# Last block's stores on ScalarE with halved copies, second loads chained from the third batch on, and a new table of priorities

## The chip, the cores and the metric

One core of one Trainium2 chip runs the whole kernel. The metric is the device time in microseconds. Shares and instruction times come from one profiled execution.

## The reference

Two stages follow each other. The first is a gated linear attention over 4 batches, 8 heads, 768 steps and 48 channels; the second takes its output, as 4 x 768 rows of 384, through a product, a three-tap convolution with a sigmoid gate, and a second product.

```python
# attention, per batch and head
for t in range(S):
    cur = (u * k_t) outer v_t
    y_t = r_t @ (state + cur)
    state = w_t[:, None] * state + k_t outer v_t
# second stage: x is y with heads side by side, (4, 768, 384)
h = relu(x @ w_in)                       # w_in 384 x 1024
c = sum over j of conv_w[j] * h shifted by j - 1 along the sequence
out = (h * sigmoid(c)) @ w_out           # w_out 1024 x 384
```

The three weights arrive as 8-byte floats.

## The kernel before

**Tiling.** The attention goes in 24 chunks of 128 steps, six for each batch. `loads` fetches a chunk's w, k, r and v on SyncE's queue (line 613); `stage_a` transposes them on TensorE (645), scans the decays on VectorE (654, 662), forms products on GpSimd (692, 694) and turns the keys back (712). `stage_b` does the state work of a chunk on TensorE: the carried part (771), the scores (803), the update (813) and the part within (781). ScalarE copies the result into `xT` (863), VectorE writes the remainder beside it (865), and after a batch's fourth and sixth chunk SyncE moves the spare rows into place with six transfers each time (874).

**Blocks.** The second stage goes in eight blocks of 384 rows, two for each batch. For each of eight f, `block` runs nine matmuls (885), then the steps of `gating`: ScalarE 897, 898, 903, 906, VectorE 899, 901, 904, GpSimd 907. The values stand in `gh` tiles, three f to a tile. Then 24 matmuls (914) for each of three output tiles sum over f; in the last block the order of those is by f first and by output tile second. A copy (945) and a store (946) end each output tile.

**Weights.** GpSimd fetches `w_in` by indirect transfers (571), SyncE loads `w_out` (584), and `from_double` and `convert` turn the words into 4-byte values with VectorE (522, 525), ScalarE (520, 542) and GpSimd (528, 543).

**Second loads for the word checks.** `again` loads the weights a second time in six pieces (602) on ScalarE's queue, and `small_words` reads each with two ScalarE operations (534) that sum up words outside the range that the fast path is made for, into the tile `flags`. Lines 1058 to 1062 turn all sums into one number, `inside`: a reduction on VectorE, a matmul on TensorE, a comparison on VectorE. Each engine then loads that number (1066) and branches (1067) over a slow path that is there for unusual inputs.

**The order** is made by `Plan`: each piece of work is handed to `op` with an engine, a length from `LEN`, what it reads and writes, and a rank. `Plan.issue` walks through a simulated time; when an engine is free it takes the ready operation with the least rank. The rank is a number for the chunk or block plus entries of the table `SHIFT`, one for the stage (`a1`, `i7`, `w1`) and one for the stage's letter with the operation's kind (`wfetch`, `pwts`, `ascan`). The result is one fixed sequence for each engine. Tiles with few copies are places of a `Kind`; `gh` tiles and the raw tiles of weights share a ring of five permits, and `Kind.take` holds a place back for a kind that still has tiles to come:

```python
kept = sum(max(0, min(o.keep - o.held, o.wanted - o.served)) for o in self.kinds if o is not self)
if self.held >= self.cap or len(self.places) <= kept:
    return None
```

Of the kernel before, what the change touches and what calls it, by code (L numbers as in the profile page):

```python
# [43 lines left out]
    fill=0.17, kh=0.335, guard=0.62, sbd=0.34, xhi=0.49, relu=0.5, mul=0.47, sig=0.43, cast=0.41, out=0.36, exp=0.46,  # L44
    z=1.03, zh=0.73, dsel=0.6, diag=1.07, lo=0.97,
    words=1.28, top=0.1, sdl=0.27, fetch=1.1, gather=1.6, rest=0.3, carried_rows=1.4, y_rows=1.5, ones=0.8,
    load=0.78, issue=0.55, spread=0.73,
)
SHAPE = dict(cross=3, half=3, output=3, scores=1, state=2, y=2, state_y=2, y_rows=2)
TURN = dict(tr=0.18, kback=0.18, carried=0.18)  # L50
PAUSE = 0.08
SHIFT = dict(
    a1=486, a10=10, a11=-18, a12=1721, a13=-81, a14=373, a15=1550, a16=-5, a17=-2983, a19=60, a2=-187, a21=-120,
    a22=-359, a23=-323, a3=564, a4=-460, a5=2857, a6=-907, a7=26, a8=-1139, adg=2121, adsel=469, afill=-1128,
    agather=278, aguard=-10, akback=101, akh=236, akt=-56, aones=259, ascan=8, asmall=202, aspread=80, atop=1,
    atr=6061, az=192, azh=-1916, b0=293, b1=54, b10=172, b11=311, b12=-289, b13=205, b14=-397, b16=-43, b17=-125,
    b18=422, b19=72, b2=8, b20=-384, b21=-277, b23=-27, b24=571, b3=-36, b4=114, b5=-77, b6=179, b8=-463, b9=123,
    bcph=2596, bcross=123, bhalf=477, boutput=378, bs=3878, bsa=-378, bsd=-16, bsdl=365, bsmall=10, bspread=-21,
    bxhih=-35, bxloh=-4306, c=-10, cexp=97, cfill=-99, cissue=-266, clo=239, ctr=191, cwords=-316, cwstt=-125,
    cwts=-21, i0=-310, i2=438, i3=-28, i5=-331, icast=-1967, igate=-1561, imm3=3579, imul=-1362, irelu=285, isig=-154,  # L60
    istt=1127, k=-26, kissue=225, ksmall=-331, l0=-133, l1=55, l11=147, l12=-694, l13=-381, l14=143, l16=-331,
    l18=213, l19=-23, l2=-167, l20=1132, l21=35, l22=-131, l23=-75, l3=-175, l4=-219, l5=-37, l7=19, l8=-366, l9=146,
    lload=5054, o0=-231, o1=195, o2=-305, o3=135, o4=-32, o5=-160, o6=-14, o7=61, oissue=-72, omm3=8366, oout=-13,
    p0=-400, p1=-1988, p10=-778, p11=-1950, p12=-115, p13=-232, p14=-285, p15=589, p16=-556, p2=16, p3=-496, p4=5592,
    p5=162, p6=315, p7=29, p9=125, pcast=963, pexp=-965, plo=-954, pwstt=1024, pwts=1129, q0=995, q2=-301, q3=1717,
    q4=-5, q5=-10, qissue=-174, qwords=273, w1=-800, w2=105, w3=606, w6=-356, wfetch=285, wissue=-178,
)
TAIL = dict(PE=0.22, DVE=0.11, ACT=0.13, POOL=0.07, SP=2.3, LOAD=1.8)
BEGIN = dict(PE=4.3, DVE=3.0, ACT=3.2, POOL=8.3, SP=0.8)
# [77 lines left out]
class Plan:  # L147
# [6 lines left out]
    def op(self, eng, us, f, r=(), w=(), holds=(), moves=0.0, port=False, rank=None):  # L154
        i, deps = len(self.ops), set()
        self.tags.append((self.stage, self.stage[0] + us))
        self.what.append(us)
        us = LEN[us] if isinstance(us, str) else us
        for t in r:
            if t in self.last:  # L160
                deps.add(self.last[t])
            self.readers.setdefault(t, []).append(i)
        for t in w:
            if t in self.last:
                deps.add(self.last[t])
            deps.update(self.readers.get(t, ()))
            self.last[t], self.readers[t] = i, []
        deps.discard(i)
        bufs = []
        for t in (*r, *w, *holds):  # L170
            if isinstance(t, Buf) and t not in bufs:
                bufs.append(t)
                t.uses += 1
                if t.turn is None:
                    t.turn = t.kind.wanted
                    t.kind.wanted += 1
        self.ops.append((eng, us, f, deps, bufs, moves, port,
                         (self.rank if rank is None else rank) + sum(SHIFT.get(x, 0) for x in self.tags[i]) + i * 1e-6))
# [191 lines left out]
def rwkv_conv_moe_kernel(  # L370
# [12 lines left out]
    nc = tc.nc  # L383
    B, H, S, D = r.shape
    DM, DF = w_in.shape
# [4 lines left out]
    NCH = S // L  # L390
# [3 lines left out]
    KT = DM // P  # L394
# [5 lines left out]
    N = B * NCH  # L400
# [48 lines left out]
    for m in range(KT):  # L449
        for g in range(2):  # L450
            half, r0 = rows_of[m][64 * g:64 * g + 64], (6 + g) * D + 16 * m - D
# [51 lines left out]
    op = plan.op  # L503
# [27 lines left out]
    def small_words(raw, buf, k, n, reads, rows=P):  # L531

        for j, kind in enumerate((U32, I32)):
            op("ACT", "words", lambda j=j, kind=kind: nc.scalar.activation(
                out=raw()[:, 0:2 * n:2].bitcast(F32), in_=raw()[:, 1:2 * n:2].bitcast(kind), func=AF.Relu, scale=-2.0 ** -30,
                bias=small_lo[0:rows, j:j + 1], accum_out=flags[0:rows, N + 2 * k + j:N + 2 * k + j + 1]),
                reads, [buf, ("flag", N + 2 * k + j)])
# [53 lines left out]
    def again(k):  # L591

        raw, n = Buf(raw_k), DF if k < KT else min(3, FT - 3 * (k - KT)) * DM

        def words():
            return raw.t.rearrange("p j c -> p (j c)")[:, 0:2 * n]
        if k < KT:
            rows, source = words, w_in[k * P:(k + 1) * P, :]
        else:
            t = 3 * (k - KT)  # L600
            rows, source = lambda: raw.t[:, 0:n // DM, :], w_out[t * P:t * P + n // DM * P, :].rearrange("(t p) c -> p t c", p=P)
        op("ACT", "issue", lambda: nc.scalar.dma_start(out=rows(), in_=source), [("x", (B - 1) % 2, NCH - 1, j) for j in range(10)], [(raw, 0)], [raw], moves=(0.0027 * n, 309.0 if k < KT else 122.0, 8))
        small_words(words, raw, k, n, [(raw, 0)])


# [275 lines left out]
    def product_in(t, f, m, x0, xs, wi=wi):  # L881

        j = 0
        for (a, c) in ((0, 0), (0, 1), (1, 0)):
            nc.tensor.matmul(t.t[:, 0:HB + 2], lhsT=wi[:, m, a, f * P:(f + 1) * P], rhs=xT[:, x0 + m, c, xs],  # L885
                             start=(m == 0 and j == 0), stop=(m == KT - 1 and j == 2))
            j += 1
# [24 lines left out]
    def product_out(acc, part, f, tt):  # L912
        for (a, c) in ((0, 0), (0, 1), (1, 0)):
            nc.tensor.matmul(acc.t[:, 0:DM], lhsT=part(a)[:, tt * P:(tt + 1) * P], rhs=wo[:, f, c, :],  # L914
                             start=(f == 0 and a + c == 0), stop=(f == FT - 1 and a == 1))

    def block(b, s0, width, base, last):
        xs = slice(s0, s0 + width + 2)
        x0 = (KT + 1) * (b % 2)
        xr = [("x", b % 2, c, j) for c in range(max(0, s0 - 1) // L, min(s0 + width, S - 1) // L + 1) for j in range(10)]  # L920
        gs = []
        for f in range(FT):
            plan.rank, plan.stage = base + f * UNIT, f"i{b * NB + s0 // HB}"
            t, a1, g = Buf(mm), Buf(a1_k), Buf(g_k)
            if f % 3 == 0:
                gh = Buf(gh_k)
            for m in range(KT):
                f0 = f * P // HB * HB
                op("PE", "mm3", lambda t=t, f=f, m=m: product_in(t, f, m, x0, xs),
                   [*xr, ("wi", m, f0), (("wi", m, f0), 1)], [t])  # L930
            key, part = ("gh", b, s0, f), lambda a, gh=gh, f=f: gh.t[:, f % 3, a, :]
            for j, (e, us, fn, rd, wr) in enumerate(gating(t, a1, g, part, f, width, key)):
                op(e, us, fn, rd, wr, [gh] if j > 5 else [], port=(e == "POOL"))
            gs.append((gh, key, part))
        plan.stage = f"o{b * NB + s0 // HB}"
        for tt in range(width // P):
            acc = Buf(mo)
            for f in range(FT):
                plan.rank = base + FT * UNIT + (f * 3 + tt if last else tt * FT + f) * DOWN
                gh, key, part = gs[f]  # L940
                op("PE", "mm3", lambda acc=acc, f=f, tt=tt, part=part: product_out(acc, part, f, tt),
                   [key, (key, 1), ("wo", f), (("wo", f), 1)], [acc], [gh])
            o = Buf(val_k)
            rows = slice(s0 + tt * P, s0 + (tt + 1) * P)
            op("ACT", "out", lambda acc=acc, o=o: nc.scalar.copy(out=o.t, in_=acc.t[:, 0:DM]), [acc], [o])
            op("SP", "issue", lambda o=o, rows=rows: nc.sync.dma_start(out=out[b, rows, :], in_=o.t), [o], [], moves=(0.6, 62.0, 8))

# [75 lines left out]
    for n in range(N + 1):  # L1023
# [29 lines left out]
    inside = const.tile([1, 1], I32, name="inside")  # L1053
# [7 lines left out]
       ["fsum"], [total])  # L1061
    op("DVE", "small", lambda: nc.vector.tensor_scalar(
        out=inside, in0=total.t[0:1, 0:1], scalar1=0.0, scalar2=None, op0=ALU.is_le), [total], ["inside"])
    plan.issue()
    fast.close()
    flag = nc.values_load(inside, min_val=0, max_val=1)
# [32 lines left out]
```

## Time and profile before

| what | us |
|---|---|
| time, median of 3 runs (342.13 to 344.29) | 343.53 |
| the profiled execution's time | 342.58 |
| its span, first to last instruction | 340.9 |
| TensorE, VectorE, ScalarE, GpSimd busy | 314.6, 262.9, 223.6, 184.1 |
| end of the last matmul for an output | 332.76 |

The time stands 1.7 us above the span. Names in the rows: PE is TensorE, PEld its weight load, DVE VectorE, ACT ScalarE, POOL GpSimd, SP SyncE; a q behind an engine's name is its queue, with transfers, waits, loads of a number and branches, which are not counted as busy. PEclk is TensorE's granted clock as a share of full speed.

### The profile page before, as it was taken

What the parts mean: (1) busy time and instruction counts of PE and PEld (TensorE: products, weight loads), DVE (VectorE), ACT (ScalarE), POOL (GpSimd) and SP (SyncE); (2) the same over time, 40 slices, a digit from 0 to 9 for tenths busy, and PEclk for the clock granted to TensorE, in tenths of its full rate; (3) what the DMA queues carried; (4) which work ended last, traced back from release to release, by engine and by line L of the source; (5) the groups of instructions that cost most, each with busy time, mean ns of one, the idle gap of its engine ahead of it and who ended that gap; (6) DMA issues with size and microseconds to landing.
All of it is one profiled execution on the core that took longest, in us unless ns stands there. A gap on an engine that the chain in (4) does not pass through costs nothing.

```text
span 340.9 us, 11473 instructions
## 1 busy us (share of the span) xinstructions
PE 314.6 (92%) x4510; PEld 294.6 (86%) x4510; DVE 262.9 (77%) x620; ACT 223.6 (66%) x587; POOL 184.1 (54%) x242
## 2 busy tenths in 40 slices
PE   8858858789999999999999999999999999999990
PEld 3846646689999999999999999999999999999990
DVE  5899998999999787698986867899998547554500
ACT  4266545987877643678866534878856348898780
POOL 8978983997674961247844621547733303413320
PEclk9998995799999999999999999999999999999996
DMA  8989864663371364368243633664501323534522
GB/s 158 322 283 213 217 168 88 127 122 66 75 155 44 84 129 102 62 125 170 65 94 77 145 52 97 129 123 104 122 17 50 91 42 125 166 126 162 180 98 79
DMA packets 114467, 41.37 MB, mean 121 GB/s; under 512 B 103117, under 2 KB 110822, under 8 KB 113638
## 3 DMA queue, kind: packets, MB, share of 16 engines
q1 hardware_dynamic: 112468, 31.14, 41.4%
q10 hardware_dynamic: 1506, 6.29, 5.4%
q0 software_dynamic: 432, 3.15, 2.4%
q8 instruction: 36, 0.59, 0.7%
q14 instruction: 25, 0.20, 0.2%
HBM read 31.48 MB, written 4.72 MB: 106 GB/s over the span
## 4 chain that ended last, share of the span: by engine, by line
PE 77%; DVE 7%; DMA 5%; POOL 3%; ACT 2%; SPq 2%; issue 1%; POOLq 0%
PE bank L914 30%; PE bank L885 28%; PE bank L645 5%; PE bank L771 3%; PE bank L781 3%; DMA gh<-in_moe_w_in_dram,limits 3%; PE bank L803 3%; PE bank L813 2%; DMA w<-in_w_dram 2%; PE bank L712 2%; POOL wide L528 1%; SPq L688 1%; DVE kr L662 1%; DVE kr L654 1%; DVE wide L525 1%
## 5 line engine op out<-in xcount | busy, mean ns | idle before, releaser
L914 PE MATMUL bank<-wo,gh 128*128 128x384 f32 x576 | 117.4, 345 | 0.0
L907 POOL TENSOR_TENSOR gh<-g,gh 128x384 fp32r<-128x384 f32 x64 | 64.7, 1018 | 95.4 <-ACT gh L906 94.7
L885 PE MATMUL bank<-xT,wi 128*128 128x386 f32 x576 | 111.3, 345 | 1.2 <-DVE xT L865 0.6
L885 PEld LDWEIGHTS bank<-xT,wi 128*128 128x128 f32 x576 | 102.8, 191 | 2.6 <-DVE kr L662 1.0
L914 PEld LDWEIGHTS bank<-wo,gh 128*128 128x128 f32 x576 | 99.0, 188 | 0.8
L899 DVE SCALAR_TENSOR_TENSOR a<-bank,cw,a 128x384 f32<-128x384 f32 x64 | 38.9, 611 | 21.4 <-ACT a L898 20.8
L897 ACT ACTIVATE bank<-bank 128x386 f32<-128x386 f32 x64 | 30.5, 481 | 23.6 <-PE bank L885 22.7
L904 DVE TENSOR_TENSOR g<-bank,a 128x384 f32<-128x384 f32 x64 | 35.0, 550 | 11.5 <-POOL gh L907 10.3
L704 POOL TENSOR_SCALAR_AFFINE_SELECT pm<-dg 64x512 f32<-64x512 f32 x46 | 30.2, 656 | 19.0 <-PE bank L781 14.1
L901 DVE SCALAR_TENSOR_TENSOR a<-bank,cw,a 128x384 f32<-128x384 f32 x64 | 38.7, 608 | 1.1 <-DVE sd L739 0.4
L906 ACT CAST gh<-g 128x384 fp32r<-128x384 f32 x64 | 32.1, 514 | 10.5 <-DVE g L904 9.7
L898 ACT ACTIVATE a<-bank,cw 128x384 f32<-128x384 f32 x64 | 37.0, 583 | 2.5 <-DVE dA L659 1.4
L903 ACT ACTIVATE a<-a 128x384 f32<-128x384 f32 x64 | 33.6, 525 | 7.3 <-DVE a L901 6.2
L692 POOL TENSOR_TENSOR z<-r,k 128x384 f32<-128x384 f32 x24 | 24.3, 1013 | 17.4 <-issue 6.1
L654 DVE TENSOR_TENSOR_SCAN kr<-bank,one_end 128x387 f32<-128x387 f32 x24 | 22.9, 956 | 4.2 <-POOL kr L480 2.7
L863 ACT CAST xT<-bank 112x256 fp32r<-112x256 f32 x48 | 16.1, 377 | 14.5 <-PE bank L781 14.3
L694 POOL TENSOR_TENSOR z<-z,ubc 128x384 f32<-128x384 f32 x24 | 24.3, 1014 | 1.0
L771 PE MATMUL bank<-kr,sa 48*48 48x64 f32 (+1 forms) x288 | 21.1, 232 | 2.5 <-DVE bank L828 1.1
L662 DVE TENSOR_TENSOR_SCAN kr<-bank,dA 128x387 f32<-128x387 f32 x24 | 22.9, 953 | 0.1
L771 PEld LDWEIGHTS bank<-kr,sa 48*48 48x48 f32 (+1 forms) x288 | 14.8, 129 | 8.4 <-issue 3.5
L528 POOL TENSOR_TENSOR wide<-wide,wide 128x384 int32<-128x384 int32 (+2 forms) x18 | 16.6, 929 | 7.2 <-DVE wide L525 6.7
L841 DVE COPY_PREDICATED pm<-upper_half,bank 128x256 f32<-128x256 int32 x48 | 20.0, 442 | 0.6 <-POOL pm L704 0.6
(106 smaller groups left out, 546.8 us busy)
## 6 DMA issues: line engine op xcount, KB each, us to landing
w<-in_w_dram SPq DMA_DIRECT2D x24, 192.0 KB, 3.5
k<-in_k_dram SPq DMA_DIRECT2D x24, 192.0 KB, 3.4
r<-in_r_dram SPq DMA_DIRECT2D x24, 192.0 KB, 3.5
v<-in_v_dram SPq DMA_DIRECT2D x24, 192.0 KB, 3.8
out_dram<-wide SPq DMA_DIRECT2D x24, 192.0 KB, 3.0
gh<-in_moe_w_in_dram ACTq DMA_DIRECT2D x3, 1024.0 KB, 4.8
gh<-in_moe_w_out_dram SPq DMA_DIRECT2D x2, 1152.0 KB, 6.3
gh<-in_moe_w_out_dram ACTq DMA_DIRECT2D x2, 1152.0 KB, 5.2
```

The source lines that it names most:

```text
L704: op("POOL", "zh", lambda p=slice(HL * j, HL * (j + 1)): nc.gpsimd.affine_select(out=pm.t[p].rearrange("p g m t -> p (g m) t"), in_=dg.t[p ...
L771: nc.tensor.matmul(to(h, m, c, w), lhsT=q["sa" if h else "sd"].t[p, m, 0:w], rhs=rt(out_of, m)[p, HL * h:HL * (h + 1)], start=first(h, c), ...
L885: nc.tensor.matmul(t.t[:, 0:HB + 2], lhsT=wi[:, m, a, f * P:(f + 1) * P], rhs=xT[:, x0 + m, c, xs], start=(m == 0 and j == 0), stop=(m == ...
L897: ("ACT", "relu", lambda: nc.scalar.activation(out=h(0, width + 2), in_=h(0, width + 2), func=AF.Relu), [t], [t]),
L898: ("ACT", "mul", lambda: nc.scalar.mul(out=a(), in_=h(1), mul=cw[:, 1, bass.ds(f, 1)]), [t, "cw"], [a1]),
L899: ("DVE", "stt", lambda: nc.vector.scalar_tensor_tensor(out=a(), in0=h(0), scalar=cw[:, 0, bass.ds(f, 1)], in1=a(), op0=ALU.mult, op1=ALU. ...
L901: ("DVE", "stt", lambda: nc.vector.scalar_tensor_tensor(out=a(), in0=h(2), scalar=cw[:, 2, bass.ds(f, 1)], in1=a(), op0=ALU.mult, op1=ALU. ...
L903: ("ACT", "sig", lambda: nc.scalar.activation(out=a(), in_=a(), func=AF.Sigmoid), [], [a1]),
L904: ("DVE", "gate", lambda: nc.vector.tensor_tensor(out=g.t[:, 0:width], in0=h(1), in1=a(), op=ALU.mult), [t, a1], [g]),
L906: ("ACT", "cast", lambda: nc.scalar.copy(out=part(0)[:, 0:width], in_=g.t[:, 0:width]), [g], [key]),
L907: ("POOL", "lo", lambda: nc.gpsimd.tensor_tensor(out=part(1)[:, 0:width], in0=g.t[:, 0:width], in1=part(0)[:, 0:width].bitcast(F32), op=AL ...
L914: nc.tensor.matmul(acc.t[:, 0:DM], lhsT=part(a)[:, tt * P:(tt + 1) * P], rhs=wo[:, f, c, :], start=(f == 0 and a + c == 0), stop=(f == FT ...
```

## The change

The last block's three output tiles are copied in halves, columns 0 to 191 by ScalarE and 192 to 383 by VectorE, and ScalarE issues their stores in place of SyncE. The second loads wait for the last chunk of the third batch, in place of the fourth; from the second of them on each waits also for the second word operation of the one before. LEN gets lengths for the new kinds of operation, and an operation `after` on GpSimd's list, which issues nothing, follows `inside`. All values of SHIFT are new.

```diff
-    load=0.78, issue=0.55, spread=0.73,
+    load=0.78, issue=0.55, outh=0.23, send=0.36, after=3.0, spread=0.73,
...
 SHIFT = dict(
-    a1=486, a10=10, a11=-18, a12=1721, a13=-81, a14=373, a15=1550, a16=-5, a17=-2983, a19=60, a2=-187, a21=-120,
...
-    agather=278, aguard=-10, akback=101, akh=236, akt=-56, aones=259, ascan=8, asmall=202, aspread=80, atop=1,
...
-    p0=-400, p1=-1988, p10=-778, p11=-1950, p12=-115, p13=-232, p14=-285, p15=589, p16=-556, p2=16, p3=-496, p4=5592,
-    p5=162, p6=315, p7=29, p9=125, pcast=963, pexp=-965, plo=-954, pwstt=1024, pwts=1129, q0=995, q2=-301, q3=1717,
-    q4=-5, q5=-10, qissue=-174, qwords=273, w1=-800, w2=105, w3=606, w6=-356, wfetch=285, wissue=-178,
+    a0=-2743, a1=1205, a10=-1850, a11=-18, a12=-6, a13=282, a14=-2337, a15=341, a16=-576, a17=-44, a18=-40, a19=93,
...
+    afill=-419, agather=102, aguard=-486, akback=1290, akh=-1246, akt=-1343, aones=-131, apad=292, ascan=140,
...
+    oissue=1003, omm3=7616, oout=-662, oouth=36, p0=-49, p10=25, p11=-97, p12=-110, p13=-148, p14=257, p15=-16,
+    p16=-26, p3=65, p4=3558, p5=-2, p6=138, p8=208, pcast=283, pexp=-1847, plo=73, pwstt=122, pwts=640, q0=-475,
+    q1=-334, q3=132, q4=1, q5=-1, qissue=-479, qwords=357, w1=-512, w3=437, w4=-1220, w5=381, w6=7, wfetch=-1128,
+    wissue=-42,
 )
...
-        op("ACT", "issue", lambda: nc.scalar.dma_start(out=rows(), in_=source), [("x", (B - 1) % 2, NCH - 1, j) for j in range(10)], [(raw, 0)], [raw], moves=(0.0027 * n, 309.0 if k < KT else 122.0, 8))
+        op("ACT", "issue", lambda: nc.scalar.dma_start(out=rows(), in_=source), [("x", (B - 2) % 2, NCH - 1, j) for j in range(10)] + [("flag", N + 2 * k - 1)] * (k >= 1), [(raw, 0)], [raw], moves=(0.0027 * n, 309.0 if k < KT else 122.0, 8))
...
             o = Buf(val_k)
             rows = slice(s0 + tt * P, s0 + (tt + 1) * P)
+            if last:
+                half = DM // 2
+                op("ACT", "outh", lambda acc=acc, o=o: nc.scalar.copy(out=o.t[:, 0:half], in_=acc.t[:, 0:half]), [acc], [o])
+                op("DVE", "outh", lambda acc=acc, o=o: nc.vector.tensor_copy(out=o.t[:, half:DM], in_=acc.t[:, half:DM]),
+                   [acc], [(o, 1)], [o])
+                op("ACT", "send", lambda o=o, rows=rows: nc.scalar.dma_start(out=out[b, rows, :], in_=o.t), [o, (o, 1)], [],
+                   moves=(0.6, 62.0, 8))
+                continue
...
+    op("POOL", "after", lambda: None, ["inside"], [])
     plan.issue()
```

## Rows read from the trace of the kernel before

**Rows 1.** The page's first part, busy us of each engine and instructions.
```profile
PE 314.6 (92%) x4510; PEld 294.6 (86%) x4510; DVE 262.9 (77%) x620; ACT 223.6 (66%) x587; POOL 184.1 (54%) x242
```

**Rows 2.** Table by stretch: length, busy us by engine, granted clock, DMA share, GB/s.
```profile
core 0: us, PE busy (x) PEld busy (x) DVE busy (x) ACT busy (x) POOL busy (x), PEclk, DMA share, GB/s
...
40.00:60.00 20.00, 14.28 (x238) 11.45 (x236) 17.50 (x47) 11.10 (x39) 13.46 (x18) 0.83 0.63 143
60.00:80.00 20.00, 17.37 (x325) 16.05 (x326) 19.16 (x48) 17.92 (x51) 19.85 (x22) 0.91 0.55 108
...
280.00:300.00 20.00, 20.00 (x116) 20.00 (x115) 12.74 (x24) 17.07 (x38) 7.06 (x7) 1.00 0.46 147
```

**Rows 3.** Chain of waits in order of time: start, us, what, near its end.
```profile
316.55 15.37 PE bank L914 x87
332.03 0.73 PE bank L914 x3
```

**Rows 4.** TensorE's groups by line from 275.75 to 332.8 us.
```profile
L914 PE MATMUL bank<-wo,gh 128*128 128x384 f32 x178 | 33.4, 338 | 0.0
L885 PE MATMUL bank<-xT,wi 128*128 128x386 f32 x144 | 27.1, 339 | 0.0
```

**Rows 5.** Timeline of the end: start, us, engine, line, operation, idle before.
```profile
332.07 0.15 DVE L1062 TENSOR_SCALAR inside<-bank 1x1 int32<-1x1 f32 x1 [1.41 <-PE bank L1060]
332.79 0.48 ACT L945 COPY wide<-bank 128x384 f32<-128x384 f32 x1 [0.35 <-PE bank L914]
```

**Rows 6.** Line 946's instructions (ns, first and last start) and landings, last and all.
```profile
L946 SPq DMA_DIRECT2D out_dram<-wide x1: 332/332/332, 333.3 to 333.3; - x1
...
DMA to landing us min/median/max: 3.8/3.8/3.8
...
DMA to landing us min/median/max: 1.9/3.0/5.7
```

**Rows 7.** Line 1067's instructions on SyncE's and VectorE's queues.
```profile
L1067 SPq EVENT_SEMAPHORE  x8: 17/17/17, 337.8 to 338.3; - x8
...
L1067 DVEq COMPARE_BRANCH  x1: 72/72/72, 332.9 to 332.9; - x1
...
L1067 SPq COMPARE_BRANCH  x1: 50/50/50, 334.6 to 334.6; - x1
L1067 DVEq EVENT_SEMAPHORE  x1: 21/21/21, 335.8 to 335.8; - x1
```

**Rows 8.** Line 1094's instructions, SyncE's next eight waits and ScalarE's joining.
```profile
L1094 SPq EVENT_SEMAPHORE  x8: 17/28/28, 338.4 to 338.9; - x8
...
L1094 ACTq EVENT_SEMAPHORE  x1: 17/17/17, 340.2 to 340.2; - x1
```

**Rows 9.** Lines 863 and 850: copies out of a bank, ns least, median, most.
```profile
L863 ACT CAST xT<-bank x48: 357/378/391, 23.1 to 274.8; 112x256 fp32r<-112x256 f32 x48
...
L850 DVE COPY sa<-bank x4: 344/346/346, 15.6 to 216.1; 112x192 f32<-112x192 f32 x4
```

**Rows 10.** Line 602's issues (ns, first and last start) and their landings.
```profile
L602 ACTq DMA_DIRECT2D gh<-in_moe_w_in_dram x3: 335/341/367, 282.2 to 294.9; - x3
...
DMA to landing us min/median/max: 4.8/5.2/6.7
```

**Rows 11.** Line 534's word operations on the second loads.
```profile
L534 ACT ACTIVATE gh<-gh,limits x12: 978/1258/1377, 289.6 to 329.3; 128x1024 f32<-128x1024 uint32 x3, 128x1024 f32<-128x1024 int32 x3, 128x1152 f32<-128x1152 uint32 x2, 128x1152 f32<-128x1152 int32 x2
L534 ACT ACTIVATION_READ_ACCUMULATOR gh<-gh,limits x12: 185/190/248, 290.8 to 330.2; 128x1 f32 x12
```

**Rows 12.** Line 874's spreads from 215 to 225 us.
```profile
L874 SPq DMA_DIRECT2D xT<-xT x6: 586/596/1167, 219.3 to 223.4; - x6
```

**Rows 13.** Waits of TensorE to 75 us and of its weight loads after.
```profile
PE bank L645 <- ACT w L639: 4.7, 3, 2.9
...
PEld bank L771 <- issue: 3.3, 14, 0.3
```

**Rows 14.** Table by stretch around 65 us, columns as in rows 2.
```profile
60.00:65.00 5.00, 3.36 (x84) 3.03 (x85) 4.72 (x11) 4.88 (x16) 5.00 (x6) 0.66 0.95 188
65.00:70.00 5.00, 4.96 (x90) 4.61 (x80) 5.00 (x14) 4.97 (x14) 5.00 (x6) 1.00 0.17 35
```

More of the change, by code (lines that the diff above doesn't have):

```diff
@@ L52 @@
 SHIFT = dict(
-    a1=486, a10=10, a11=-18, a12=1721, a13=-81, a14=373, a15=1550, a16=-5, a17=-2983, a19=60, a2=-187, a21=-120,
-    a22=-359, a23=-323, a3=564, a4=-460, a5=2857, a6=-907, a7=26, a8=-1139, adg=2121, adsel=469, afill=-1128,
-    agather=278, aguard=-10, akback=101, akh=236, akt=-56, aones=259, ascan=8, asmall=202, aspread=80, atop=1,
-    atr=6061, az=192, azh=-1916, b0=293, b1=54, b10=172, b11=311, b12=-289, b13=205, b14=-397, b16=-43, b17=-125,
-    b18=422, b19=72, b2=8, b20=-384, b21=-277, b23=-27, b24=571, b3=-36, b4=114, b5=-77, b6=179, b8=-463, b9=123,
@@ L58 @@
[L58 to L62, printed above, removed]
@@ L63 @@
-    lload=5054, o0=-231, o1=195, o2=-305, o3=135, o4=-32, o5=-160, o6=-14, o7=61, oissue=-72, omm3=8366, oout=-13,
-    p0=-400, p1=-1988, p10=-778, p11=-1950, p12=-115, p13=-232, p14=-285, p15=589, p16=-556, p2=16, p3=-496, p4=5592,
-    p5=162, p6=315, p7=29, p9=125, pcast=963, pexp=-965, plo=-954, pwstt=1024, pwts=1129, q0=995, q2=-301, q3=1717,
-    q4=-5, q5=-10, qissue=-174, qwords=273, w1=-800, w2=105, w3=606, w6=-356, wfetch=285, wissue=-178,
+    a0=-2743, a1=1205, a10=-1850, a11=-18, a12=-6, a13=282, a14=-2337, a15=341, a16=-576, a17=-44, a18=-40, a19=93,
@@ new lines @@
+    a2=-120, a20=-286, a21=-368, a23=-53, a3=69, a4=-225, a5=176, a6=22, a7=-19, a8=-453, a9=140, adg=3465, adsel=218,
+    afill=-419, agather=102, aguard=-486, akback=1290, akh=-1246, akt=-1343, aones=-131, apad=292, ascan=140,
+    asmall=89, aspread=4, atop=437, atr=5190, az=1575, azh=37, b0=199, b1=-2481, b10=-814, b12=-24, b13=-109, b14=40,
+    b15=42, b16=-4, b17=252, b18=-338, b19=50, b2=-494, b21=-171, b22=-126, b23=177, b24=-212, b3=-769, b4=-596,
+    b5=152, b6=141, b7=-571, b8=187, b9=5, bcph=5108, bcross=-2438, bhalf=-533, boutput=-9, bs=5972, bsa=-43,
@@ new lines @@
+    bsd=-1832, bsdl=146, bsmall=19, bspread=47, bxhih=-1439, bxloh=-2970, c=227, cexp=1, cfill=-78, cissue=276,
+    clo=-236, ctr=40, cwords=6, cwts=266, i0=-536, i1=-447, i2=-371, i3=-601, i4=-93, i5=672, i7=-453, icast=-847,
+    igate=-2463, ilo=1229, imm3=3677, imul=-570, irelu=787, istt=1491, k=-4, kissue=-111, ksmall=221, l0=-960,
+    l1=-678, l10=3, l11=146, l12=1, l14=-1208, l15=-307, l16=142, l17=220, l19=594, l2=-34, l21=-423, l22=-2, l23=374,
+    l3=122, l4=291, l5=53, l6=15, l8=84, l9=58, lload=6157, o0=25, o1=-775, o2=-73, o3=-70, o5=-219, o6=-40, o7=247,
```

## The prediction

> **What bounds the kernel now.** I read the busy shares first [rows 1]: TensorE 92%, VectorE 77%, ScalarE 66%. The table by stretch shows where the missing TensorE time lies [rows 2]: it is busy 14.28 of the 20 us from 40 on and 17.37 of the next, the granted clock is 0.83 and 0.91 there, and VectorE (17.50, then 19.16) and GpSimd (up to 19.85) are the full ones. In the late stretch TensorE stands at 20.00 of 20, at clock 1.00. The chain of waits tells the same of the end [rows 3]: line 914 runs 87 matmuls in 15.37 us, 0.177 us each, and the last three end at 332.03 + 0.73 = 332.76. After 275.75 there are 144 matmuls of line 885 and 178 of line 914 [rows 4]; 322 x 0.177 = 57.0 us is all of 332.76 - 275.75. There is no hole to close in that stretch.
>
> So I treat the span as three terms: a ramp of about 74 us, a TensorE-filled middle whose length is its work, and a tail from the last matmul T = 332.76 to 340.9, that is 8.14 us. An edit pays only if it shortens the ramp, takes work or shape changes from TensorE, or shortens the tail.
>
> **The tail, step by step.** Before: the last copy starts at 332.79 and takes 0.48 [rows 5]; SyncE issues that store at 333.3, T + 0.53, and it lands 3.8 us later [rows 6], at 337.1. SyncE itself is late beside it: it comes to the flag only after its last issue, branches at 334.6 and executes its next instruction, the first of eight waits, at 337.8 [rows 7], 3.2 us behind the branch. VectorE spends 2.9 us on the same step (332.9 to 335.8), and no other work ends then. From SyncE's 337.8 to the end are 3.1 us, in which the engines join at 340.2 [rows 8].
>
> After: the three last stores leave SyncE. It can load the flag and take its branch as soon as the flag is there, and the 3.2 us run beside the matmuls, provided that the flag is early (next part). What is late next is the last store's landing, and two new things lie ahead of it.
>
> The copies. On ScalarE 384 columns take 0.48 [rows 5] and 256 columns 0.378, on VectorE 192 columns take 0.346 [rows 9]; by the slope of ScalarE's two, 192 columns are 0.33 us there, an estimate. A half copy saves 0.15 us, not half.
>
> The issue. One of ScalarE's own transfers occupied its queue 0.34 to 0.37 us [rows 10], and it must wait for both halves. So one output tile costs ScalarE about 0.33 + 0.06 + 0.36 = 0.75 us (the 0.06 is my allowance for the handover), while the three tiles' matmuls end 3 x 0.177 = 0.53 us apart. Before, copies alone took 0.48 of each 0.53. The queue now falls behind: with the first tile ready at T - 1.06, the last store is issued at about T + 0.8 if the halves run side by side, against T + 0.53. What stands behind the waiting issue on ScalarE is the next tile's half copy and the flag load; VectorE waits for nobody.
>
> No row shows ScalarE and VectorE reading one bank at once: their steps on a bank, the copy of line 863 and the subtraction of line 865 say, follow each other. If the halves are kept one behind the other, each tile needs 0.35 + 0.06 more, part of it in ScalarE's idle time, and the last issue is at about T + 1.3. I take T + 1.0, between the two. The Trainium skill (PSUM — Partial Sum Buffer, PSUM bank collisions raise a hardware error) says that two engines must be kept apart on the same bank and quadrant, reads included; by that the halves go one after the other and the sum would end 0.3 us later than mine, otherwise 0.2 earlier.
>
> The landing is 3.0 us by the median of the 24 stores [rows 6]; I bound it by the least, 1.9, and by the last one's 3.8. SyncE's remainder is 3.1 us if all its sixteen waits [rows 7, 8] stand behind the landing, and 2.0 (from 338.9) if all have passed; I take 2.6. Sum: 1.0 + 3.0 + 2.6 = 6.6 against 8.14, a gain of **1.5 us**. The upper end, 1.3 + 3.8 + 3.1 = 8.2, is no gain; the lower, 0.8 + 1.9 + 2.0 = 4.7, is about where VectorE sets a floor: its last half ends near T + 0.4, 0.7 to the branch (332.22, the flag, to 332.9), the 2.9, and 0.7 of closing from 340.2 on. So the tail gives 0 to 3.4 us.
>
> **The second loads.** The first is issued at 282.2 [rows 10], the twelve word operations start from 289.6 to 329.3 [rows 11], and the flag is written at 332.07 + 0.15 [rows 5]. The new condition is the third batch's last chunk, whose spreads are issued from 219.3 to 223.4 [rows 12], so about 226. One link of the chain is a landing of 4.8 to 6.7 us [rows 10] and two operations of 1.26 + 0.19 [rows 11], thus 7.7 to 9.6; the first load waited 2.6 us more for ScalarE (landed 287.0, read at 289.6). Six links of 10.3 to 12.2 us end at 288 to 299, and some 2 us from the last word to the flag follow. That is over 30 us ahead of T.
>
> Where this goes: ScalarE loses 12 x 1.45 = 17.4 us of work between 289 and 331, where it was 17.07 of 20 busy [rows 2], but TensorE did not wait for it there, so I cost that at nothing. The same 17.4 us, and the transfers, arrive at 226 to 300 and can stand ahead of the copies and spreads of the last batch's chunks. The cover is the backlog: of the work after 275.75, 178 - 72 of line 914 and 72 of line 885 need no last chunk, 178 x 0.177 = 31 us. A delay of 17.4 us is hidden, with 14 to spare; what goes beyond would be paid in full. A load's raw tile takes a permit of the ring of five; one permit is held back for raw tiles as long as any is still to come, so the blocks have four before and after. The flag's matmul moves along TensorE's queue at an unchanged cost.
>
> **The shifts.** The whole table of priorities is new, so all queues are laid out anew, SyncE's and GpSimd's too. I can follow only a few. At GpSimd's head, fetch 1 (285 - 800 before, -1128 - 512 after) still precedes chunk 0's products. On VectorE the conversion of the first piece (1129 - 400, now 640 - 49) passes chunk 1's scan (8 + 486, now 140 + 1205), whose own rank differs by little. That makes block 0's weights earlier and chunk 1 later; the rows don't say which is worth more. I bound the ramp's change by TensorE's longest single wait in it, 2.9 us [rows 13], each way. For the middle, TensorE shows fourteen gaps of 0.24 us each, 3.3 in all, on entering the state work of line 771 [rows 13]; half as many more or fewer is 1.7 us. I take zero for both, for want of a sign.
>
> `after`, `outh` and `send` in LEN, and the operation on POOL that does nothing, add no instruction; they only move the planner's end.
>
> **The rivals.**
> The new order shortens the ramp: one wait of 2.9 us less beside the tail, 339.1. For it speaks that 8.3 us of TensorE time are idle between 40 and 80 alone and that the clock is low there; against it that VectorE and GpSimd are full in that stretch and keep the same work.
> The new order lengthens the ramp by the same: 344.9.
> The ramp gets longer and the low clock stays. From 60 to 65 us the granted clock is 0.66, a mean between the levels of 1.2 and 2.4 GHz, and TensorE is busy 3.36 of 5; from 65 on it is busy 4.96 at 1.00 [rows 14]. If chunk 1's later scan opens a gap just there, these 4.96 us run at 0.66: 4.96 x (1/0.66 - 1) = 2.6, and with the 2.9 the kernel ends at 347.5. It decides as soon as the clock's return falls behind 70 us.
> The tail gives nothing, since the store lands at the upper end or the flag isn't early (a link waits for a permit): 343.5.
>
> **How the numbers follow.** The profiled execution took 342.58, its span 340.9 and 1.68 around it; less 1.5 it would be 341.1. The median of the three runs is 343.53, 0.95 above, and my time is on that scale: 343.5 - 1.5 = **342.0**. Chances: forecast, with the order worth less than 1.9 us either way, 0.40; shorter ramp 0.32; longer ramp 0.11; no gain 0.05; low clock 0.12. The range takes in the shorter ramp with nearly all of the tail's other bound (339.1 - 1.6 = 337.5) and the longer ramp with the halves in turn (344.9 + 0.3, and as much for the middle): 337.5 to 345.5. A change of 1% (3.4 us) is about what a measurement here can tell from none. Faster than 340.1 is the shorter ramp, 0.32; slower than 346.9 the low clock, 0.12; the rest is 0.56.
>
> **What the changed profile would show.** The tail: SyncE's flag load before T, no 3.2 us of SyncE behind the last matmul, the last store's issue on ScalarE's queue at T + 0.8 to 1.3, and 6.6 us from T to the end. The second loads: first issue near 226, each behind the words of the one before, the flag near 300. The middle: no hole on TensorE between 275 and T. The ramp: the first stretch with TensorE at 20.00 of 20, and the clock rows before it; T itself, 332.76 now, sums up all that the order does. I am wrong if T moves by more than 2 us, if a landing on ScalarE's queue is outside 1.9 to 3.8, or if the flag is late.

## The result, and the profile after

The changed kernel took 346.09 us (median of 22 runs, 343.17 to 352.18), the kernel before 343.71 in the same rounds: ratio **1.0064, interval 1.0043 to 1.0084**, so 2.2 us slower by the ratio (1.5 to 2.9) and 2.4 by the medians. The forecast was 342.0, in a range that ended at 345.5. Medians are over all runs of a kernel; ratios and intervals leave out its slow runs, those more than 1.5% above its fastest (three of these 22, and nine of twelve of the changed kernel with its loads in pieces of 512 bytes, below).

The profiled execution of after took 347.86, its span 345.9. That is 1.8 above its median, where before's profile is 1.1 below its own; so two traces that differ by 5.0 us in span stand for a difference of 2.2 to 2.4.

The page's first part, to be held against [rows 1]:

```profile
PE 317.8 (92%) x4510; PEld 296.6 (86%) x4510; DVE 265.5 (77%) x623; ACT 222.8 (64%) x587; POOL 184.3 (53%) x242
```

The same matmuls, three more operations on VectorE, and TensorE busy 3.2 us longer. Nothing in it says why.

**The end** came as forecast. Timeline of after near its end: start, us, engine, line, operation, idle before.

```profile
339.06 0.36 DVE L949 COPY wide<-bank 128x192 f32<-128x192 f32 x1 [11.67 <-PE bank L915]
339.46 0.32 ACT L948 COPY wide<-bank 128x192 f32<-128x192 f32 x1 [11.13 <-DVE wide L949]
339.60 0.36 DVE L949 COPY wide<-bank 128x192 f32<-128x192 f32 x1 [0.17 <-PE bank L915]
...
340.27 0.56 ACT L948 COPY wide<-bank 128x192 f32<-128x192 f32 x2 [0.50 <-DVE wide L949]
```

The halves go one after the other: ScalarE's waits until VectorE's is done. The last matmul ends at T = 340.10 (chain below), and line 951, ScalarE's issue, and line 1077, the branch (1067 before), show the rest. Instructions of these lines on each queue, with first and last start:

```profile
L951 ACTq DMA_DIRECT2D out_dram<-wide x3: 362/370/388, 339.8 to 341.1; - x3
```

```profile
L1077 SPq EVENT_SEMAPHORE  x8: 17/17/17, 341.7 to 344.4; - x8
...
L1077 SPq COMPARE_BRANCH  x1: 50/50/50, 328.7 to 328.7; - x1
...
L1077 DVEq COMPARE_BRANCH  x1: 72/72/72, 340.8 to 340.8; - x1
...
L1077 DVEq EVENT_SEMAPHORE  x1: 21/21/21, 344.2 to 344.2; - x1
```

Last issue at T + 1.0; SyncE's branch long before T, in place of 334.6 [rows 7]; the last of its eight waits 3.3 us behind that issue, and 1.5 from there to the end: 5.8 against 8.14.

**The middle** did not. T itself is 7.3 us later than 332.76 [rows 3]. Chain of waits of after in order of time (start, us, what):

```profile
270.86 1.24 SPq L689
272.14 6.60 DMA last<-kr
278.87 0.34 PE bank L804 x5
...
280.36 1.08 PE bank L915 x3
...
282.08 1.26 PE bank L915 x3
...
320.48 19.62 PE bank L915 x111
340.12 0.37 DVE wide L949
```

The sixth of the small transfers that the last chunk's scores (804) need was issued at 272.14 and took 6.60 us to land. In the kernel before, the six of this chunk (line 688 there) took:

```profile
DMA to landing us min/median/max: 2.0/2.8/3.7
```

Timeline of after in that moment, a start and a length again:

```profile
268.31 4.42 SPq L689 DMA_DIRECT2D last<-kr  x6
...
271.32 0.38 ACTq L603 DMA_DIRECT2D gh<-in_moe_w_out_dram  x1
```

In the midst of these six ScalarE issued the fifth second load, 1152 KB beside 16.2 KB each. The table by stretch shows what TensorE made of it (length, TensorE's busy us with its matmuls, granted clock, DMA share, GB/s):

```profile
core 0: us, PE busy (x), PEclk, DMA share, GB/s
230.00:240.00 10.00, 9.28 (x155) 1.00 0.89 225
275.00:280.00 5.00, 3.15 (x127) 1.00 0.72 175
280.00:285.00 5.00, 5.00 (x94) 0.66 0.14 45
```

A hole of 1.85 us, then 5 us at a granted clock of 0.66, a mean between the levels of 1.2 and 2.4 GHz, which cost about another 5 x 0.34 = 1.7 (an estimate); and 0.72 at 230 to 240, under the first load. In the kernel before these three stretches are:

```profile
230.00:240.00 10.00, 10.00 (x124) 1.00 0.51 109
275.00:280.00 5.00, 5.00 (x30) 1.00 0.14 33
280.00:285.00 5.00, 5.00 (x31) 1.00 0.37 108
```

The 0.72 came about by a longer way. The first load was issued at 227.0; a small transfer of line 689, at 227.38, took 5.37 us to land, and the engine that stood for it was ScalarE:

```profile
232.77 0.34 ACT L743 ACTIVATE sd<-s,last 112x48 f32<-112x48 f32 x1 [1.90 <-DMA last<-kr]
```

ScalarE's gating step 904 stands behind it in its sequence; VectorE's 905 waited 1.55 us for 904, and TensorE's scores 0.54 for 905.

What was left on TensorE at 290 us, in the kernel before and then in the kernel after (TensorE's groups by line; count, then busy us and mean ns):

```profile
L914 PE MATMUL bank<-wo,gh 128*128 128x384 f32 x165 | 30.6, 338 | 0.0
L885 PE MATMUL bank<-xT,wi 128*128 128x386 f32 x76 | 14.8, 340 | 0.0
```

```profile
L915 PE MATMUL bank<-wo,gh 128*128 128x384 f32 x162 | 29.9, 338 | 0.0
L886 PE MATMUL bank<-xT,wi 128*128 128x386 f32 x120 | 22.8, 340 | 0.0
```

241 matmuls against 282. The 41 more, at the 0.177 us that one takes [rows 3], are 7.3 us, all of T's move. From 290 on both run without a hole: the loss lies ahead of it. TensorE's idle time from 75 to 290 us is 3.3 of the 7.3, and the lower clock at 280 about 1.7; the remaining 2.3 are no idle time behind 75 us.

### The profile page after: what moved, and what is told of

It reads as the page before. It is cut to its first block, busy times and chain, and to the rows that moved or that the text cites. A ratio compares the mean times of both kernels' runs of the same rounds, so it can differ in the third digit from the quotient of the medians.

```text
span 345.9 us, 11481 instructions
## 1 busy us (share of the span) xinstructions
PE 317.8 (92%) x4510; PEld 296.6 (86%) x4510; DVE 265.5 (77%) x623; ACT 222.8 (64%) x587; POOL 184.3 (53%) x242
## 3 DMA queue, kind: packets, MB, share of 16 engines
q10 hardware_dynamic: 1938, 6.88, 6.0%
## 4 chain that ended last, share of the span: by engine, by line
PE 61%; DMA 12%; DVE 8%; POOL 8%; issue 4%; ACT 3%; SPq 2%; POOLq 0%; DVEq 0%; ACTq 0%
PE bank L915 25%; PE bank L886 23%; DMA last<-kr 5%; PE bank L646 4%; DMA r<-in_r_dram 3%; PE bank L772 2%; SPq L689 2%; DMA gh<-in_moe_w_in_dram,limits 2%; DMA gh<-in_moe_w_out_dram 2%; PE bank L804 2%; PE bank L782 2%; POOL wo L544 2%; PE bank L814 2%; POOL wide L529 1%; POOL pm L705 1%
## 5 line engine op out<-in xcount | busy, mean ns | idle before, releaser
L915 PE MATMUL bank<-wo,gh 128*128 128x384 f32 x576 | 120.2, 348 | 0.2 <-POOL gh L908 0.2
L772 PE MATMUL bank<-kr,sa 48*64 48x64 f32 (+1 forms) x288 | 21.7, 236 | 3.2 <-DVE bank L829 1.4
L772 PEld LDWEIGHTS bank<-kr,sa 48*64 48x64 f32 (+1 forms) x288 | 15.1, 132 | 9.3 <-issue 3.9
L772 PE MATMUL bank<-kr,sd 48*48 48x64 f32 (+1 forms) x240 | 18.4, 237 | 4.5 <-DVE bank L829 2.8
L866 DVE TENSOR_TENSOR xT<-bank,xT 112x256 fp32r<-112x256 f32 x48 | 18.1, 414 | 3.3 <-ACT xT L864 3.1
```

The costliest lines, as they stand in the source:

```text
L772: nc.tensor.matmul(to(h, m, c, w), lhsT=q["sa" if h else "sd"].t[p, m, 0:w], rhs=rt(out_of, m)[p, HL * h:HL * (h + 1)], start=first(h, c), ...
```

## The experiments

The theory after this profile: the second loads, moved to where the last chunks' small transfers run, make these land late, and TensorE stands since its order is fixed. Rivals: the word operations on ScalarE; the new table of priorities. Each kernel was run against the kernel before on the same chip; both medians stand beside each ratio.

**Only the end changed** (the kernel before with the new copies and issues; old table, old loads).

```diff
+            if last:
+                half = DM // 2
+                op("ACT", "outh", lambda acc=acc, o=o: nc.scalar.copy(out=o.t[:, 0:half], in_=acc.t[:, 0:half]), [acc], [o])
...
+                op("ACT", "send", lambda o=o, rows=rows: nc.scalar.dma_start(out=out[b, rows, :], in_=o.t), [o, (o, 1)], [],
```

> The kernel before with only the last block's halved copies and ScalarE's stores; second loads and priorities as before. Theory (the tail is a gain, the loss lies elsewhere): T stays at 332.8, the flag stays late (332.2), SyncE branches near 333.3 instead of 334.6, and the kernel ends 1 to 1.5 us earlier, 342.2 to 342.7 against 343.7. Rival (the stores on ScalarE's queue eat the gain): 343.7 or slower.

342.72 against 344.25, ratio 0.9964 [0.9942, 0.9987]. Faster by 1.2 us by the ratio (0.4 to 2.0), 1.5 by the medians, though the flag was still late. Line 1075, the branch there:

```profile
L1075 SPq EVENT_SEMAPHORE  x8: 17/17/17, 336.8 to 338.6; - x8
...
L1075 SPq COMPARE_BRANCH  x1: 50/50/50, 333.7 to 333.7; - x1
```

With T at 333.2 the tail is 6.9: the 3.1 us behind SyncE's branch now run beside the last store's landing. After's tail is 1.1 shorter: its last issue is at T + 1.0 where here it is at T + 1.3, and its landing takes 3.3 where here it takes 4.1. How much of that the early flag makes, these two traces don't separate.

**The change with the old table.**

```diff
 SHIFT = dict(
-    a0=-2743, a1=1205, a10=-1850, a11=-18, a12=-6, a13=282, a14=-2337, a15=341, a16=-576, a17=-44, a18=-40, a19=93,
...
+    a1=486, a10=10, a11=-18, a12=1721, a13=-81, a14=373, a15=1550, a16=-5, a17=-2983, a19=60, a2=-187, a21=-120,
```

> The changed kernel with the old table of priorities, so the order up to about 220 us is that of before. Theory (the second loads hold up the transfers last<-kr of the last chunks, and TensorE, whose order is fixed, stands still for them): TensorE shows idle time between 225 and 290 us waiting for last<-kr, T is 2 to 5 us later than 332.8, and with the tail's 2.3 us the time is 343.5 to 346.5. Rival (the new priorities carry all of the loss): no idle time there, T at 332.8, the time 341.4.

348.16 against 344.25, 1.0076 [1.0038, 1.0113], above the theory's range. The loads harm the old order too, elsewhere. Its chain of waits:

```profile
227.82 6.75 DMA w<-in_w_dram
...
274.31 4.08 DMA last<-kr
```

Here the first load was issued 0.5 us behind a chunk's load of w, at 228.32, and TensorE was busy 21.80 of the 25 us from 225 on. The new table isn't what makes the loads cost.

**The change with thin second loads**: same order on every engine, an eighth of each load moved and read (seven eighths of the check left out).

```diff
-            rows, source = words, w_in[k * P:(k + 1) * P, :]
+            rows, source = lambda: words()[:, 0:n // 4], w_in[k * P:(k + 1) * P, 0:n // 4]
...
-        small_words(words, raw, k, n, [(raw, 0)])
+        small_words(words, raw, k, n // (8 * (n // DM if k >= KT else 1)), [(raw, 0)])
```

> The changed kernel with its order untouched, but the second loads move only a part of their columns and the word operations read only that part, so most words go unchecked the second time. Theory (second loads): the landing of last<-kr near 272 us falls from 6.6 to about 2 us, TensorE has no idle time after 225 us, T falls by 3.5 to 5 us, and the time is 341 to 342.5 against 346.1 of the changed kernel. Rival (new priorities): the time stays within 1 us of 346.

342.81 against 344.25, 0.9974 [0.9952, 0.9995]. The same two stretches:

```profile
230.00:240.00 10.00, 10.00 (x163) 1.00 0.57 116
275.00:280.00 5.00, 5.00 (x135) 1.00 0.40 91
```

Both holes are gone, T falls from 340.1 to 334.2, and the tail is 5.8 as in after. Against before that is -0.9 us by the ratio where the change has +2.2: bytes and words of the loads together cost 3.1 us (by the medians, -1.4 and +2.4, 3.8).

**Only the new table** (the kernel before with the new SHIFT).

```diff
-    a1=486, a10=10, a11=-18, a12=1721, a13=-81, a14=373, a15=1550, a16=-5, a17=-2983, a19=60, a2=-187, a21=-120,
...
+    a0=-2743, a1=1205, a10=-1850, a11=-18, a12=-6, a13=282, a14=-2337, a15=341, a16=-576, a17=-44, a18=-40, a19=93,
```

> The kernel before with the new table of priorities alone; second loads, copies and stores as before. Theory (two thirds of the loss are the second loads, one third the ramp): at 90 us TensorE is about 2.3 us of work behind the kernel before, no more is lost later, T is near 335 and the time 346, as the tail has no gain. Rival (all from the second loads): T near 332.8 and the time 343.7. Rival (all from the priorities): T near 337.5 and 348.4.

345.80 against 344.25, 1.0046 [1.0023, 1.007], T at 337.2. The order alone costs 1.6 us (0.8 to 2.4). Not all of that need be in the changed kernel: from 330 to 337 us TensorE stands 0.9 us here for gating, with ScalarE's words (535) between the gating steps in the chain, and in after the words are over by then. The time came as the theory had it, T as the rival had it that blames the priorities alone.

**Whole loads, thin words**: the last edit of the thin loads alone, so that all bytes move and an eighth of the words is read.

```diff
-        small_words(words, raw, k, n, [(raw, 0)])
+        small_words(words, raw, k, n // (8 * (n // DM if k >= KT else 1)), [(raw, 0)])
```

> The changed kernel with its order untouched and the second loads whole, but the word operations read only a part of the words, so ScalarE's 17.4 us mostly go and the transfers stay. Theory (the transfers do the harm): the time stays at 345.5 to 347, TensorE still stands idle between 225 and 290 us behind a landing. Rival (ScalarE's word operations stand ahead of the state work's copies): the time falls to 342.8, as with thin transfers.

347.90 against 343.98, 1.0123 [1.0088, 1.0158]: no better than the change itself. The loads are issued at nearly the same times, 227.4 to 284.4 against 227.0 to 284.6, and taking out most of ScalarE's 17 us of word operations gained nothing. (No run has thin bytes and whole words.) TensorE's longest wait from 75 us on is now for another small transfer:

```profile
PE bank L804 <- DMA xT<-xT: 1.8, 1, 1.8
```

**The old priorities for the early stages only** (weights, chunks 0 to 5, blocks 0 and 1), the new ones for the rest; the kernel before otherwise.

```diff
+        part, at = self.stage[0], int(self.stage[1:] or 0)
+        shift = OLD if part in "wpc" or part in "lab" and at < 6 or part in "io" and at < 2 else SHIFT
```

> The kernel before with the new priorities for chunks from 6 and blocks from 2 on, and the old ones for the weights, the chunks 0 to 5 and the blocks 0 and 1; nothing else of the change. Theory (the new order's loss is the ramp, where VectorE puts weight conversions around the scans of chunk 4 and 5): those scans start at 52 and 67.6 us again instead of 54.5 and 70.7, and the time is 343.7 to 344.5 against 345.8 of the new priorities alone. Rival (the loss lies in the middle and late part): 345.3 to 346.5.

358.16 against 343.98, 1.0407 [1.037, 1.0444]. Mixing made an order worse than either: the scan that should start at 67.6 us started at 75.0, where both parents have it by 70.8. Nor did the edit do what the theory needs. The two scans that it names are the seventh and the eighth in VectorE's order, so those of chunks 6 and 7, counted from 0, and the edit leaves chunks from 6 on with the new priorities. It says nothing on the ramp.

**Whole copies on VectorE**, stores on ScalarE; a single run.

```diff
-                op("ACT", "outh", lambda acc=acc, o=o: nc.scalar.copy(out=o.t[:, 0:half], in_=acc.t[:, 0:half]), [acc], [o])
...
+                op("DVE", "out", lambda acc=acc, o=o: nc.vector.tensor_copy(out=o.t, in_=acc.t[:, 0:DM]), [acc], [o])
```

> The changed kernel with whole copies of the last block's tiles on VectorE; stores still on ScalarE's queue. Theory (the halves run one behind the other, 0.36 + 0.32 us and two handovers): one copy of 0.5 to 0.55 us takes less time than both, the last issue is at T + 0.6 to 0.7 instead of T + 1.0, and from T to the end are 5.3 to 5.6 us instead of 5.8. Rival (VectorE's own branch, 3.4 us behind its last copy, sets the end): 5.8 to 6.1.

346.96 beside a median of 343.98. Its timeline and its branch, line 1074:

```profile
338.31 1.62 DVE L947 COPY wide<-bank 128x384 f32<-128x384 f32 x3 [11.67 <-PE bank L915]
```

```profile
L1074 SPq EVENT_SEMAPHORE  x8: 17/17/17, 340.8 to 343.5; - x8
...
L1074 DVEq COMPARE_BRANCH  x1: 72/72/72, 340.3 to 340.3; - x1
...
L1074 DVEq EVENT_SEMAPHORE  x1: 21/21/21, 343.7 to 343.7; - x1
```

T is 339.35 and the tail 5.75, as with halves. VectorE is ready 3.4 us behind its own branch and 0.2 us behind SyncE's last wait for the store; in after it is 0.2 ahead of that wait. From SyncE's last wait to the end are 1.6 us here and 1.5 in after, so VectorE's 0.2 cost nothing that shows. Halving the copies is worth nothing that a trace shows.

**An early flag in the old order**: the end changed as in the first experiment, the loads waiting for the last chunk's own rows alone and put first on ScalarE.

```diff
-    q4=-5, q5=-10, qissue=-174, qwords=273, w1=-800, w2=105, w3=606, w6=-356, wfetch=285, wissue=-178,
+    q4=-5, q5=-10, qissue=-9000, qwords=-3000, w1=-800, w2=105, w3=606, w6=-356, wfetch=285, wissue=-178,
```

> The kernel before with its old priorities, the new tail, and the second loads moved forward only as far as the last chunk's own rows, first in line on ScalarE and for permits. Theory (the flag is worth about 1 us when it is early, and loads that start after the last chunk's transfers hold up nothing): flag near 315 us, no idle time on TensorE behind a landing, 5.8 us from T to the end, the time 341.3 to 342.3. Rival (word operations in a row stop the gating of the last blocks): TensorE waits for gating between 300 and 330, the time 343 or more.

346.67 against 343.98, 1.0084 [1.0055, 1.0113]. SyncE's branch came to 327.4 and the tail to about 6.1, but words in a row held up the gating, as the rival had it. TensorE's waits from 270 us on:

```profile
PE bank L1068 <- DVE fsum L1066: 1.6, 1, 1.6
PE bank L914 <- ACT gh L906: 0.7, 1, 0.7
```

The first is the flag's own matmul: it stands in TensorE's fixed order, and all behind it waited for VectorE's reduction, which the chain of waits puts behind ScalarE's word operations (534).

**Second loads in pieces of 512 bytes**, in the change and in the change with the old table: is it the long rows or the bytes?

```diff
+        part = w_in[k * P:(k + 1) * P, :] if k < KT else w_out[3 * (k - KT) * P:3 * (k - KT) * P + n // DM * P, :]
+        source = part.rearrange("r c -> (r c)").rearrange("(j p c) -> p j c", p=P, c=P)
+        rows = lambda: words().rearrange("p (j c) -> p j c", c=P)
```

> The changed kernel, same order, same bytes of the second loads, but cut into pieces of 512 B (which row lands where differs; every word is still read). Theory A (the long rows of 8 and 9 KB hold the transfer engines, and the small pieces of chunk loads and of last<-kr wait behind them): landings on SyncE's queue near 272 us return to about 2 us, the holes go, the time falls to 342.8 as with thin transfers. Theory B (it is the bytes, whatever their pieces): the time stays at 346 to 348, with TensorE's holes.

> The changed kernel with the old priorities, and the second loads in pieces of 512 B. Theory A: no hole at 225 to 250 us, T near 333, 5.8 us from T to the end, the time 341 to 342. Theory B: 346 to 349, as with whole rows (348.2).

Medians 351.83 for the first and 347.15 for the second, against 344.10; ratios 1.0084 [1.0028, 1.0139], from the three runs of the first that it keeps, and 1.0112 [1.0065, 1.0158], where whole rows had 1.0064 and 1.0076. No gain in either. The long rows alone are not the cause; that it is the bytes, whatever their pieces, is argued and not shown. The pages count 4754 packets on ScalarE's queue in place of 1938 for the same 6.88 MB, so the packets became 2.5 times smaller, not 512 bytes. By the Trainium skill (DMA: Bandwidth & Descriptors, Queues, rings and completion order) each transfer engine takes turns between queues packet by packet, which had made smaller pieces worth a try; neither run shows a benefit.

**The table switched at 72 us of the planner's time**, old before and new behind it, and the reverse.

```diff
+                table = FIRST_TABLE if t < 72.0 else SHIFT
+                for i in sorted(ready[e], key=lambda i: self.ops[i][7] + sum(table.get(x, 0) for x in self.tags[i])):
```

> The kernel before, its order made with the old priorities up to 72 us of planned time and with the new ones after. Theory (the new priorities lose in the ramp): the scans of chunk 4 and 5 start at 52 and 67.6 us, and the time is 343.5 to 344.5. Rival (they lose later): 345 to 346.5.

> The kernel before, its order made with the new priorities up to 72 us of planned time and with the old ones after. Theory (the ramp): chunk 5's first scan at 70 to 71 us, T later by about 2 us, the time 345 to 346.5. Rival (the loss lies later): 343.5 to 344.5.

355.47 and 348.52 against 344.10: 1.0357 [1.0318, 1.0395] and 1.0139 [1.0104, 1.0175]. The first kept the old ramp (the eighth scan, the expectation's chunk 5, at 67.6 us); of the 12 us that its T is later, TensorE's idle time in this stretch behind it is 4.7:

```profile
120.00:200.00 80.00, 75.32 (x1100) 0.96 0.43 89
```

So a mixture is again worse than either whole, and these runs can't say what part of the new table costs.

**Only the fifth load thin**, and **only the fifth load whole**; the order is that of after.

```diff
+            cut = DM // 4 if k == 4 else 2 * DM
+            rows, source = lambda: raw.t[:, 0:n // DM, 0:cut], w_out[t * P:t * P + n // DM * P, 0:cut].rearrange("(t p) c -> p t c", p=P)
```

> The changed kernel, same order; only the fifth second load and its word operations are cut to a part of their columns, so most of its words go unchecked. Theory (the fifth, issued between the last chunk's transfers, makes the hole at 276 to 279 us and the lower clock behind it): that hole goes, 2.5 to 3.5 us are won, the time is 342.8 to 343.8. Rival (the six share the loss evenly): 0.6 us won, 345.5 to 346.5.

> The complement: the fifth second load whole, the five others cut to a part of their columns, so most of their words go unchecked; same order. Theory: the hole at 276 to 279 us stays, the time is 345 to 346. Rival (even shares): 343 to 344.

344.25 and 344.55 against 343.61: 1.0018 [0.9995, 1.0041] and 1.004 [1.0011, 1.007]. The two stretches of the first, then of the second:

```profile
230.00:240.00 10.00, 9.45 (x157) 1.00 0.88 226
275.00:280.00 5.00, 5.00 (x159) 1.00 0.41 68
```

```profile
230.00:240.00 10.00, 10.00 (x161) 1.00 0.63 129
275.00:280.00 5.00, 3.68 (x135) 1.00 0.55 106
280.00:285.00 5.00, 5.00 (x72) 1.00 0.23 72
```

Each hole goes with its own loads. Both times lie between their theory and their rival. By the ratios the fifth out saves 2.2 - 0.6 = 1.6 us and the five others out 2.2 - 1.4 = 0.8; by the medians it is 1.8 and 1.5. With intervals of some 0.8 us and more on each side, that doesn't tell which share is larger. The clock did not fall behind the second one's hole of 1.32 us.

**The fifth and sixth loads later**, behind the last chunk's own rows; nothing is left out.

```diff
-        op("ACT", "issue", lambda: nc.scalar.dma_start(out=rows(), in_=source), [("x", (B - 2) % 2, NCH - 1, j) for j in range(10)] + [("flag", N + 2 * k - 1)] * (k >= 1), [(raw, 0)], [raw], moves=(0.0027 * n, 309.0 if k < KT else 122.0, 8))
+        op("ACT", "issue", lambda: nc.scalar.dma_start(out=rows(), in_=source), [("x", (B - 2 + (k >= 4)) % 2, NCH - 1, j) for j in range(2 if k >= 4 else 10)] + [("flag", N + 2 * k - 1)] * (k >= 1), [(raw, 0)], [raw], moves=(0.0027 * n, 309.0 if k < KT else 122.0, 8))
```

> The changed kernel; the fifth and sixth second loads wait for the last chunk's own rows, as early as these are written. Theory: no hole on TensorE at 276 to 279 us, the flag still well before T, 5.8 us of tail, the time 342.5 to 343.8. Rival (what is moved stands ahead of the last blocks' gating instead): 345 or more.

344.36 against 343.61, 1.0005 [0.9977, 1.0034], the median a little above the theory's 343.8. T is 335.5, and the late stretch is whole:

```profile
275.00:280.00 5.00, 5.00 (x201) 1.00 0.46 100
```

It undoes the change's loss but not more. The best full version measured stays the one with only the end changed, 0.9964.

## Why the prediction was wrong

**The tail was right**, and a little more than forecast: 2.3 us of 8.14 gained, where I had 1.5 (0 to 3.4). The issue is at T + 1.0, as taken. The halves run in series, 0.36 on VectorE, then 0.32 on ScalarE, which waits for VectorE's. The Trainium skill (PSUM — Partial Sum Buffer, PSUM bank collisions raise a hardware error) wants two engines kept apart on one bank and quadrant, and the trace agrees. Yet the queue got no later than T + 1.0, since ScalarE's part of one tile runs beside VectorE's of the next. Landing and remainder were 3.3 + 1.5 = 4.8 in place of 3.0 + 2.6; the 1.5 is less than the 2.0 that I took for the least. VectorE's next instruction, in my floor of 4.7, comes at T + 4.1 (344.2), 0.2 ahead of SyncE's last wait for the store (344.4), so that the store's landing and VectorE's branch are nearly even.

**The chain of the second loads ran on time**: first issue at 227.0 (about 226), flag at 298.1 (about 300), SyncE's branch before T. What follows was wrong.

**The step that failed is "The cover is the backlog"**, with "a delay of 17.4 us is hidden". The backlog was there: 282 matmuls of lines 915 and 886 at 290 us. But it could not be used. TensorE's sequence is fixed by the planner, and the last chunk's scores stand in it ahead of that backlog; when their keys land late, TensorE stands before them with some 50 us of work queued behind them. So cover is only what stands in the queue ahead of the waiter. And I priced the wrong thing: ScalarE's 17.4 us of words, whose removal gained nothing (thin words), and not the transfers, which I named ("and the transfers") and gave no term. A row for it was in reach: these loads had taken 4.8 to 6.7 us to land [rows 10], at a DMA share of 0.46 in a stretch that holds three of them [rows 2], and the new place of the loads is that of the last chunks' transfers [rows 12]. The runs put it, with the words, at 3.1 us by the ratios and 3.8 by the medians.

**The zero for the order** was mis-sized too, by about 1.5 us: 1.6 from the table alone, with the reservation made there; 1.4 if the change's +2.2 is the sum of -2.3 (tail), +3.1 (loads) and the rest (0.9 by the medians). So the sign was that of the rival with the longer ramp, at half its 2.9. The start of the sequence differs as follows. VectorE's seventh pair of scans (chunk 6 counted from 0, the expectations' chunk 4) in the kernel before, then after:

```profile
52.13 0.96 DVE L654 TENSOR_TENSOR_SCAN kr<-bank,one_end 128x387 f32<-128x387 f32 x1 [0.62 <-PE bank L645]
...
53.42 0.96 DVE L662 TENSOR_TENSOR_SCAN kr<-bank,dA 128x387 f32<-128x387 f32 x1
```

```profile
54.25 0.96 DVE L655 TENSOR_TENSOR_SCAN kr<-bank,one_end 128x387 f32<-128x387 f32 x1
55.12 0.54 DVE L523 TENSOR_SCALAR bank<-gh 128x384 int32<-128x384 int32 x1
...
55.77 0.56 DVE L526 SCALAR_TENSOR_TENSOR wide<-gh,bank 128x384 int32<-128x384 int32 x1
...
56.71 0.95 DVE L663 TENSOR_TENSOR_SCAN kr<-bank,dA 128x387 f32<-128x387 f32 x1
```

Weight conversions (523, 526) pass between the scans, and the second starts 3.3 us later; in the next two pairs it is 3.0 and 6.1. That this is the cause of the order's loss is argued and not shown: the three kernels that mixed the tables were all worse than both. Which part of the table costs stays open. Of my two readings on the table, one didn't come and one was wrong: chunk 1's scan, which I expected to be passed by a conversion, starts at 10.00 against 9.98; and the fourteen gaps of [rows 13] are those of weight loads, which run beside the matmuls, while the matmuls of the kernel before show no wait from 75 us to T, so my 1.7 us for the middle had no ground.

**The low clock** came, but not where that rival had it, at 65 to 70 us (1.00 there): it came behind the hole at 275 to 280, as a part of the loads' price, and in the profiled ramp ahead of 65:

```profile
45.00:50.00 5.00, 3.70 (x78) 0.50 0.56 173
```

It is 0.50 up to 60 us, where before has 1.00, 0.62 and 0.69 in the three stretches of 5 us. From 40 to 60 us the mean is 0.63 in after and 0.83 before; five variants of after that change only its loads or words (both thin, thin words, the three on the fifth load) had 0.76 to 0.84. So this belongs to the profiled execution more than to the order. My own sign of being wrong, T moved by more than 2 us, spoke: it moved by 7.3 in these two profiles.

## What to carry to other kernels

Where each engine runs a fixed sequence, a late landing is covered only by the work that stands ahead of its waiter in the queue; a backlog behind the waiter covers nothing, however long. A load that is moved has a price beside whatever small transfers run there: look at who waits for those, not only at the engine that issues it or reads it. Taking the last stores and a late branch off one queue paid at once, alone; the early flag behind it was worth about one microsecond at most, and the loads moved for it cost more than that.

## What the runs showed of the hardware that was not expected

- A load of 1152 KB, issued amid transfers of 16.2 KB, went with 6.60 us from issue to landing for the last of these, where the same chunk's took 2.0 to 3.7 in the kernel before; with the old table a chunk's load of 192 KB took 6.75, where 3.5 is the median in the kernel before. Pieces of 512 bytes did not help.
- After a hole of 1.85 us the granted clock was 0.66 over the next 5 us, and two groups of three matmuls took 1.08 and 1.26 us in place of 0.53: the clock cost about as much as the hole. After the hole of 1.32 us in the run with only the fifth load whole, it stayed at 1.00.
- Behind its branch SyncE's next instruction came 2.9 to 3.2 us later where the flag was late (the kernel before, only the end changed, only the new table), VectorE's 2.9 to 3.5, ScalarE's and GpSimd's 0.4 to 0.8.
